# A new issue order, smaller first groups and a first chunk in two token halves, in a sketched attention with a rational activation

## The chip, the cores and the metric

The kernel runs on one core of a Trainium2 chip. The metric is the device time of one execution in microseconds, lower is better. Before the change it was 251.48 us, the median of three runs (251.42 to 254.35).

An execution profiled by the hardware gives the trace. Its span (248.8 us before) is a little shorter than the device time. The engines are called PE (matrix engine, TensorE), PEld (its weight loads), DVE (VectorE), ACT (ScalarE), POOL (GpSimd) and SP (the queue that issues most loads).

## The reference, cut to what matters

```python
def phi(x):                                   # attention with sketched features, r = 8
    a = np.einsum('rd,bhsd->bhsr', S1, x)
    b = np.einsum('rd,bhsd->bhsr', S2, x)
    return np.einsum('bhsi,bhsj->bhsij', a, b).reshape(*x.shape[:-1], r * r)
q_p, k_p = (phi(q), phi(k))                   # batch 4, heads 4, seq 1088, head_dim 32
kv  = np.einsum('bhsf,bhsd->bhfd', k_p, v)
num = np.einsum('bhsf,bhfd->bhsd', q_p, kv)
den = np.einsum('bhsf,bhf->bhs', q_p, np.sum(k_p, axis=2))[..., None] + 1e-06
x = num / den                                 # then 4352 tokens x 128
...
h = x @ w_in                                  # 128 -> 2048
P = a[0] + a[1] * h + a[2] * h2 + a[3] * h3
Q = 1.0 + np.abs(b[0]) * np.abs(h) + np.abs(b[1]) * h2
out = (P / (Q + 1e-06)) @ w_out               # 2048 -> 128
```

## The kernel before

The tokens are cut into nine chunks, eight of 512 tokens and a remainder of 256. For each chunk the queries' feature products, the division and a transpose give x; then 16 slices of 128 hidden columns are made. The slices are taken in groups, usually of eight, so that a group is 128 x 4096 elements in bfloat16. The rational function of a group is worked out in these steps:

```python
# PE:  h = w_in.T @ x, two slices (1024 columns) at a time;  ACT or DVE: hb <- h (cast, "e")
# DVE: u = |hb| (ab);  s = hb*hb (sq);           DMA or DVE: u += s             (us)
# DVE: t = a3*hb + a2 (hi);  t *= s (cu);  hb = a1*hb + a0 (lo);  DMA or DVE: t += hb   (ts)
# ACT: L = Ln(scale*u + 1);  u = Exp(-L)         (= 1/Q)
# DVE: t *= u (ov)                               (= P/Q)
# PE:  out += w_out.T @ t (pj)
```

A sum is either a DVE instruction or a DMA that accumulates, issued from GpSimd's queue. A table decides:

```python
def add(dst, src, name):
    d, s = T[dst, g][:, :gw], T[src, g][:, :gw]
    if ENGINE.get(name) == "DVE":
        nc.vector.tensor_add(out=d, in0=d, in1=s)
    else:
        nc.gpsimd.dma_start(out=d, in_=s, accum_op=AX.add, max_dma_last_dim=4096)
```

All work is a list of named steps. A fixed permutation, found by a search outside the kernel, says in which order the steps are issued; each engine then works through its own in that order:

```python
FIRST = [4, 4, 8]        # slices in the first chunk's groups;  LAST = [8, 4, 4] for the remainder
SKIP = ["f3"]
ORDER = [27, 4, 26, 30, 0, 36, ...]            # cut: 589 numbers
...
for i in order:
    s = self.steps[i]
    for key in s["take"]:
        self.slot[key] = free[key[0]].pop(0)   # a buffer of the pool
    s["fn"]()                                  # issues the instructions
```

Among the steps are dummy matmul pairs ("f0", "f1", ...), two products of 128 x 512 with zeros, 0.43 us a pair. They keep PE busy where it would stand still; a name in SKIP leaves one out.

## Time and profile before

| | before |
|---|---|
| device time, median of 3 | 251.48 us |
| span of the profiled run | 248.8 us |
| busy: PE, DVE, ACT | 222.5, 225.4, 213.7 us |
| first wide DVE operation / first logarithm | 24.68 / 32.59 us |
| last hidden matmul ends / last Exp ends | 217.3 / 243.1 us |

No engine is busy all the time and none is idle for long, so this table alone names no bound. The views have to be cut by time. The prediction shows the main cut. One more is needed, the stretches in which PE is full (start and end, length, busy time and count for PE, PEld, DVE, ACT, POOL, then granted clock, DMA share, GB/s):

```profile
50.00:110.00 60.00, 59.39 (x489) 33.49 (x490) 55.70 (x45) 54.26 (x40) 10.64 (x9) 1.00 0.99 192
110.00:200.00 90.00, 87.42 (x630) 46.22 (x629) 88.23 (x67) 86.68 (x59) 19.09 (x15) 1.00 0.97 178
```

PE has 0.6 us to spare from 50 to 110, while DVE and ACT have 4.3 and 5.7. From 110 to 200 the spare times are 2.6, 1.8 and 3.3. And at the end DVE waits for DMA sums (waits of DVE after 220 us: total us, times, longest):

```profile
DVE t L621 <- DMA t<-hb: 1.8, 4, 0.7
```

### The profile page before, as it was taken

The page shows a single profiled execution, that of the slowest core. Times are in us where ns is not written, and L with a number is a line of the kernel's source. Part 1 is how long each engine was busy: PE and PEld are TensorE (multiplying, and loading weights), DVE is VectorE, ACT ScalarE, POOL GpSimd, SP SyncE. Part 2 cuts the span into 40 slices and gives each one's busy share as a digit, 9 for nine tenths or more (in the row PEclk, how much of TensorE's full clock was granted, in tenths as well). Part 3 has the DMA queues.
Part 4 walks back from the last instruction along what each step waited for, and adds up shares of the span by engine and source line. Part 5 has one row for each costly group of instructions (what it writes and reads, how often), then busy time and mean ns, then how long its engine had stood idle before and what let it go on. Part 6 is the DMA issues. An engine that isn't in the chain of part 4 may idle for free.

```text
span 248.8 us, 4279 instructions
## 1 busy us (share of the span) xinstructions
PE 222.5 (89%) x1789; PEld 127.1 (51%) x1789; DVE 225.4 (91%) x205; ACT 213.7 (86%) x158; POOL 48.8 (20%) x61
## 2 busy tenths in 40 slices
PE   7999999999999999998999899999998969920763
PEld 2674455654636465553657354546453627720532
DVE  0785999998989989998999999999999999998993
ACT  3335589989989798989999999899999899899990
POOL 4000422132101212121111221122031312113210
PEclk9999999999999999999999999999999999995599
DMA  5994498999998899979999999999999999999982
GB/s 149 315 278 172 72 147 173 174 219 185 176 169 182 147 192 223 232 166 173 169 177 202 171 171 171 211 169 171 189 172 186 182 201 187 179 184 186 200 162 68
DMA packets 23427, 45.11 MB, mean 181 GB/s; under 512 B 5232, under 2 KB 13552, under 8 KB 23408
## 3 DMA queue, kind: packets, MB, share of 16 engines
q0 software_dynamic: 11232, 34.87, 79.7%
q1 hardware_dynamic: 11712, 9.90, 12.6%
q8 instruction: 14, 0.23, 0.4%
q10 hardware_dynamic: 464, 0.08, 0.2%
q14 instruction: 5, 0.04, 0.0%
HBM read 8.79 MB, written 2.23 MB: 44 GB/s over the span
## 4 chain that ended last, share of the span: by engine, by line
DVE 31%; PE 31%; DMA 20%; ACT 10%; issue 8%; SPq 0%; DVEq 0%; ACTq 0%; POOLq 0%
PE h_ps L572 15%; DMA u<-s 12%; DVE t L621 7%; DVE s L582 6%; DMA t<-hb 5%; DVE t L607 4%; DVE u L585 4%; PE h_ps L499 4%; ACT u L618 4%; DVE t L603 3%; PE out_ps L629 3%; ACT L L614 3%; DVE hb L610 2%; ACT hb L184 2%; DMA q<-in_q_dram 2%
## 5 line engine op out<-in xcount | busy, mean ns | idle before, releaser
L572 PE MATMUL h_ps<-xT,w_in_sb 128*128 128x512 f32 (+1 forms) x288 | 126.0, 577 | 4.2 <-ACT hb L184 2.7
L572 PEld LDWEIGHTS h_ps<-xT,w_in_sb 128*128 128x128 f32 x288 | 51.7, 190 | 56.5 <-issue 43.1
L184 ACT CAST hb<-h_ps 128x1024 bf16<-128x1024 f32 x66 | 64.8, 1020 | 8.2 <-PE h_ps L572 7.8
L614 ACT ACTIVATE L<-u,one_ap,lsc 128x4096 f32<-128x4096 bf16 (+2 forms) x20 | 65.9, 3295 | 6.4 <-DMA u<-s 6.3
L618 ACT ACTIVATE u<-L 128x4096 bf16<-128x4096 f32 (+2 forms) x20 | 62.3, 3116 | 0.2
L629 PE MATMUL out_ps<-w_out,t 128*128 128x128 bf16 x544 | 35.2, 225 | 15.8 <-DVE t L621 15.7
L594 POOL DMA_DIRECT2D u<-s x19 | 24.1, 1269 | 118.9 <-DVE u L585 54.5
L629 PEld LDWEIGHTS <-t 128*128 128x128 bf16 x544 | 32.5, 101 | 23.8 <-DVE t L621 20.6
L621 DVE TENSOR_TENSOR t<-t,u 128x4096 bf16<-128x4096 bf16 (+2 forms) x20 | 39.2, 1968 | 4.0 <-ACT u L618 2.2
L582 DVE TENSOR_TENSOR s<-hb 128x4096 bf16<-128x4096 bf16 (+2 forms) x20 | 39.2, 1963 | 1.5 <-ACT hb L184 1.5
L607 DVE TENSOR_TENSOR t<-t,s 128x4096 bf16<-128x4096 bf16 (+2 forms) x20 | 39.3, 1967 | 0.3
L594 POOL DMA_DIRECT2D t<-hb x18 | 21.6, 1200 | 72.2 <-issue 20.1
L610 DVE TENSOR_SCALAR hb<-hb,a_sb 128x4096 bf16<-128x4096 bf16 (+2 forms) x20 | 23.8, 1189 | 0.2
L603 DVE TENSOR_SCALAR t<-hb,a_sb 128x4096 bf16<-128x4096 bf16 (+2 forms) x20 | 23.6, 1183 | 0.0
L585 DVE TENSOR_SCALAR u<-hb 128x4096 int16<-128x4096 int16 (+2 forms) x20 | 22.3, 1115 | 0.1
L499 PE MATMUL h_ps<-qT,Srep 64*128 64x512 f32 (+1 forms) x72 | 19.5, 617 | 0.4 <-ACT hb L184 0.4
L506 DVE TENSOR_TENSOR q_pT<-A_sb,h_ps 128x1024 f32<-128x1024 f32 (+1 forms) x9 | 10.4, 1157 | 2.6 <-ACT A_sb L184 1.4
L519 PEld LDWEIGHTS h_ps<-kv,q_pT 128*64 128x64 f32 (+1 forms) x288 | 8.7, 134 | 5.1 <-issue 2.0
L519 PE MATMUL h_ps<-kv,q_pT 128*64 128x66 f32 (+1 forms) x288 | 10.1, 224 | 0.0
L184 ACT COPY A_sb<-h_ps 128x1024 f32<-128x1024 f32 (+1 forms) x9 | 8.7, 965 | 0.8 <-PE h_ps L499 0.8
L499 PEld LDWEIGHTS h_ps<-qT,Srep 64*128 64x128 f32 x72 | 5.4, 184 | 6.9 <-ACT hb L184 2.1
L184 ACT COPY kT<-h_ps 128x512 f32<-128x512 f32 x5 | 2.9, 585 | 5.3 <-PE h_ps L383 4.8
(89 smaller groups left out, 137.0 us busy)
## 6 DMA issues: line engine op xcount, KB each, us to landing
u<-s POOLq DMA_DIRECT2D x15, 1024.0 KB, 8.6
t<-hb POOLq DMA_DIRECT2D x15, 1024.0 KB, 9.5
k_sb<-in_k_dram SPq DMA_DIRECT2D x4, 512.0 KB, 4.3
q<-in_q_dram SPq DMA_DIRECT2D x8, 256.0 KB, 4.9
v<-in_v_dram SPq DMA_DIRECT2D x4, 512.0 KB, 8.2
out_dram<-oT SPq DMA_DIRECT2D x8, 256.0 KB, 7.0
w_in_sb<-in_moe_w_in_dram SPq DMA_DIRECT2D x2, 512.0 KB, 4.8
u<-s POOLq DMA_DIRECT2D x2, 512.0 KB, 7.7
```

Of the source, the lines that this page charges most:

```text
L184: nc.scalar.copy(out=out, in_=in_)
L499: nc.tensor.matmul(pair(i)[:, g, :W], lhsT=Srep[i][rows].rearrange("p g f -> p (g f)"), rhs=T["qT", n][rows, :W], start=True, stop=True)
L572: nc.tensor.matmul(p[:, i * W:(i + 1) * W], lhsT=w_in_sb[:, fi * 128:(fi + 1) * 128], rhs=T["xT", n][:, :W], start=True, stop=True)
L582: nc.vector.tensor_mul(out=new("s", g)[:, :gw], in0=h, in1=h)
L585: nc.vector.tensor_scalar(out=new("u", g)[:, :gw].bitcast(mybir.dt.int16), in0=T["hb", g][:, :gw].bitcast(mybir.dt.int16), scalar1=0x7FFF, ...
L594: nc.gpsimd.dma_start(out=d, in_=s, accum_op=AX.add, max_dma_last_dim=4096)
L603: nc.vector.tensor_scalar(out=new("t", g)[:, :gw], in0=T["hb", g][:, :gw], scalar1=a_sb[:, 3:4], scalar2=a_sb[:, 2:3], op0=AX.mult, op1=AX ...
L607: nc.vector.tensor_mul(out=T["t", g][:, :gw], in0=T["t", g][:, :gw], in1=T["s", g][:, :gw])
L614: nc.scalar.activation(out=new("L", g, l0)[:, :lw], in_=T["u", g][:, l0:l0 + lw], func=ACT.Ln, bias=one_ap, scale=lsc)
L618: nc.scalar.activation(out=T["u", g][:, l0:l0 + lw], in_=T["L", g, l0][:, :lw], func=ACT.Exp, scale=-1.0)
L621: nc.vector.tensor_mul(out=T["t", g][:, :gw], in0=T["t", g][:, :gw], in1=T["u", g][:, :gw])
L629: nc.tensor.matmul(T["out_ps", n][:, j * 128:(j + 1) * 128], lhsT=T["t", g][:, c:c + 128], rhs=W_out[:, fis[i], :], start=fis[i] == 0 and ...
```

## The change

The intent is to start the wide work earlier and to fit the steps together better. The first chunk is divided, transposed, evacuated and multiplied by its first two slices of w_in in two halves of 256 tokens; the first groups are 2, 2, 4 and 8 slices instead of 4, 4 and 8; a branch that no list used is removed; and the permutation, the table of engines and the buffers' homes are new. They come from a search outside the kernel.

```diff
-FIRST = [4, 4, 8]
+FIRST = [2, 2, 4, 8]
 ENGINE = {
...
-    "k31.ea": "DVE", "q7.ev": "DVE", "q8.xe": "DVE", "g1.ts": "DVE", "o0.eT": "DVE", "o1.eT": "DVE", "g7.e4": "DVE",
-    "o3.eT": "DVE", "o5.eT": "DVE", "g13.e4": "DVE", "g17.us": "DVE", "g18.ts": "DVE", "o8.eT": "DVE",
...
+    "k30.ea": "DVE", "k31.ev": "DVE", "q6.xe": "DVE", "q8.ev": "DVE", "q8.A": "DVE", "q8.xe": "DVE", "g1.us": "DVE",
+    "g1.ts": "DVE", "g6.e6": "DVE", "g17.us": "DVE", "o7.eT": "DVE", "g18.us": "DVE", "g20.us": "DVE",
+    "g20.ts": "DVE", "o8.eT": "DVE",
-FOUR = []
-SKIP = ["f3"]
+SPLIT = [0]
+SKIP = ["f2", "f10", "f8"]
 ORDER = [
-    27, 4, 26, 30, 0, 36, 1, 31, 6, 56, 20, ...      (cut: all 589 steps)
+    26, 30, 7, 1, 0, 27, 70, 71, 31, 32, 33, ...     (cut: all 604 steps)
...
+        if n in SPLIT:
+            out = []
+            for i in range(2):
+                s = plan.add(f"{nm}.dv{i}", "DVE", 830, lambda i=i: divide(i), ...)          (cut)
+                s = plan.add(f"{nm}.xt{i}", "PE", 250, lambda i=i: x_transposes(i), ...)     (cut)
+                out.append(add_copy(f"{nm}.xe{i}", lambda i=i: x_evac(i), W // 2, ...))      (cut)
+            return out
...
+            if n in SPLIT and fis[s] == 0:
+                hm = plan.add(f"{nm}.i{s}", "PE", 880, lambda s=s: h_mm(s, 0), ...)          (cut)
+                hm = plan.add(f"{nm}.h{s}", "PE", 880, lambda s=s: h_mm(s, 1), ...)          (cut)
```

Because the first chunk has one group more, a group g2 or later of the kernel before has a number one higher in the changed kernel. The last full group is g17 of the changed kernel and g16 of the one before.

## The prediction

> **What bounds the kernel now.** I read the page's busy table first, then busy time by stretch, then the chain of waits at the start, then the waits of each engine in the middle and at the end. The columns of the table are the busy time, its share of the span, and the number of instructions.
>
> ```profile
> PE 222.5 (89%) x1789; PEld 127.1 (51%) x1789; DVE 225.4 (91%) x205; ACT 213.7 (86%) x158; POOL 48.8 (20%) x61
> ```
>
> No single engine is the bound: three lie within 12 us of each other. Stretches separate them (start and end, length, busy time of each engine, granted clock, DMA share, GB/s):
>
> ```profile
> 0.00:24.68 24.68, 22.92 (x250) 13.62 (x251) 13.89 (x34) 9.69 (x15) 2.69 (x23) 1.00 0.75 230
> 24.68:50.00 25.32, 25.18 (x204) 13.96 (x204) 25.11 (x24) 20.95 (x22) 6.85 (x6) 1.00 0.87 142
> 50.00:220.00 170.00, 163.98 (x1232) 91.72 (x1232) 163.62 (x125) 160.23 (x109) 33.41 (x27) 1.00 0.98 184
> 220.00:243.10 23.10, 8.56 (x79) 6.30 (x80) 21.37 (x23) 22.86 (x13) 5.89 (x6) 0.70 0.99 185
> 243.10:248.80 5.70, 1.86 (x31) 1.52 (x28) 1.39 (x3) 0.00 (x0) 0.00 (x0) 1.00 0.16 46
> ```
>
> The cuts are chosen: 24.68 is where VectorE (DVE) begins its first wide operation, 243.10 is where ScalarE (ACT) finishes its last Exp. DVE is idle 24.68 - 13.89 = 10.8 us before the first wide operation, 0.2 in the second stretch, 6.4 in the third, 1.7 in the fourth, and 4.3 in the last. ACT is idle 15.0, 4.4, 9.8, 0.2 and 5.7. A narrower cut of the third stretch shows PE busy 59.4 of 60 us from 50 to 110 and DVE 107.9 of 110 from 110 to 220: the matrix engine sets the pace first, DVE afterwards, ACT in the last 23 us. The start is a chain, in order of time (start, length, what):
>
> ```profile
> 1.24 4.68 DMA q<-in_q_dram
> ...
> 11.16 2.48 PE h_ps L421 x80
> ...
> 15.10 1.09 PE h_ps L519 x32
> ...
> 17.70 0.59 PE h_ps L535 x4
> 18.29 1.06 PE h_ps L499 x4
> 19.35 0.62 PE w_ps L392 x16
> 19.97 7.08 PE h_ps L572 x16
> ```
>
> Two loads, then PE without a gap: the key sums (L421), the query sums (L519), the transposes of x (L535), and only after 1.7 us of the next chunk's work the first hidden matmuls (L572). In the middle ACT waits chiefly for one thing, the sum that a DMA makes before the logarithm; DVE waits for several small ones (total us, times, longest):
>
> ```profile
> ACT L L614 <- DMA u<-s: 5.7, 7, 1.2
> ACT hb L184 <- PE h_ps L572: 3.7, 6, 0.9
> ```
> ```profile
> DVE t L621 <- ACT u L618: 2.2, 4, 0.7
> DVE q_pT L506 <- PE h_ps L499: 1.2, 2, 0.7
> DVE den L526 <- PE h_ps L519: 1.1, 2, 0.7
> DVE a_t L186 <- PE w_ps L392: 1.0, 1, 1.0
> ```
>
> **What the Trainium skill says.** "Perfetto Trace Analysis", section "Optimization Strategy", says that the most-contended engine can change between regimes of a kernel, and that gaps should be looked for inside the regime concerned. The trace agrees: PE, then DVE, then ACT. "VectorE: DVE Perf Modes", section "The TRN2 errata", says that an instruction pays a fixed cost whatever its size, so cutting work smaller costs instructions. The trace agrees: the DVE product takes 2.285 us for 4096 columns, 1.215 for 2048 and 0.687 for 1024, a line with 0.16 us at zero. "DMA: Bandwidth & Descriptors", section "Issuing engines are not separate DMA queues", says that transfers of all issuers run on the same 16 engines and interleave. The trace agrees in that the DMA share is 0.98 in the middle while a 1 MB sum lands a median of 8.6 us (u) or 9.5 us (t) after issue; it rules nothing out.
>
> **The change part by part.** I read the built order of both programs.
>
> *Dead code.* The branch for FOUR is removed; its list was empty. Cost 0.
>
> *First chunk in halves, groups 2, 2, 4, 8.* One more group: three products at 0.16 us fixed, one absolute value at 0.15, two linear operations at 0.28 (0.807 us at 2048 columns against 0.543 at 1024), together +1.2 us on DVE; one more Ln and Exp, 0.38 + 0.20 = +0.6 on ACT. The divide in two adds one add, one reciprocal and one multiply of fixed cost, +0.5 on DVE; the second scaled evacuation +0.2 on ACT. Hidden matmuls in halves are neutral: 4 of 256 columns took 0.9 us against 1.72 for the whole pair.
>
> *Work moved between engines.* To DVE: three x evacuations (3 x 0.745), one cast (1.215), the remainder queries' two evacuations (0.43 + 0.68), one output (0.68), two small ones (0.98); and sums taken from DMA: one of 4096 columns (2.28), one of 2048 (1.22), four of 1024 (2.76). From DVE: one x (0.745), two casts (2.43), four outputs (2.73), two query copies (1.37), two small ones (0.71), sums of 2048, 2048 and 1024 (3.14). Net 12.5 - 11.1 = +1.4. With the parts above DVE gains 3.1 us of durations. Neighbours on DVE start about 0.07 us before the one ahead ends, and there are nine more instructions, so some +2.4 of time. ACT by the same count gets +1.4 + 0.8 = +2.2. DMA loses 5120 columns of sums, 1.3 MB of 34.9, nearly all in the last 40 us.
>
> *Start.* The loads begin with q1 (256 KB), then k0 (512), then q0 (256). From before: k0 landed near 4.9 and q0 near 5.9, so 256 KB take about 1 us; now k0 should land near 5.9 and q0 near 6.9. The keys' two transposes straddle q0's, w_in's second half and k1 go ahead of v0, and the key sums should start at 12.3 to 13.3 instead of 10.99. Then: key sums 2.7, an expansion 1.1 (which covers the two spread copies), first query sums to 16.6, x halves, g0's first half at 19.6, a transpose, q2 and q1's sums 1.9, g0's second half to 23.1, cast to 24.1. First wide DVE operation at about 24.4, against 24.68, with about the same DVE work behind it. So the halves give DVE almost nothing, because the loads take back what they save. ACT gains more: g1's sum is now on DVE, so its Ln can start after about 4.5 us of DVE work, near 29, against 32.59. That is some 2.5 us less idle ACT, about what its added work costs.
>
> *Middle.* Here the new order should pay. Between a group's last cast and its Ln, ACT has other work queued; I summed it from the order with the trace's durations (cast 1.02, Ln 3.81, Exp 3.63, copies 0.3 to 1.0). Over the ten full groups of chunks 3 to 7: mean 14.5 us before (13.1 to 17.6), 19.0 now (15.9 to 21.8). What must fit is DVE's absolute value and square (1.22 + 2.28) plus the landing (8.6, up to 12.4), 12 to 16 us: before falls short at times, as its seven waits show; now it rarely should. Most of the 5.7 us should go, and part of the 2.2 us behind it on DVE. From 24 to 110 us, where PE is full, five dummy matmul pairs (0.43 us each) stood in the order, now none: 2.2 us of PE, less about 1.3 lost at the start.
>
> *End.* DVE waited 1.8 us for the t sums; with 1.3 MB less to move I expect half. The 5.7 us from the last Exp to the end stay.
>
> *Sum.* ACT: +2.2 work, -2.5 start, -5 middle = -5. DVE: +2.4 work, 0 at the start, -3 of 6.4 in the middle, -1 at the end = -1.6. PE until 110: -0.9. The smallest gains decide, since each engine is the bound somewhere: about -1.9 us.
>
> **The rivals.** *A: added DVE work eats everything.* DVE is at 98% from 110 on, and takes a 2.28 us sum there. For: the stretch table. Against: 6 us of its idle time are still to be had. Result 251 to 253. *B: the ordering works throughout,* all ACT and most DVE waits vanish, and the start gains a microsecond because loads land sooner than I count. For: the 4.5 us of added distance. Against: DVE would need nearly no idle time outside start and end. Result 245 to 247. *C: the start gets worse,* v0 lands after 13.3 and all else shifts by 1 to 2 us. For: k1 and half of w_in before v0. Against: the share of DMA over the first 24.68 us was only 0.75. Result 251 to 252.5.
>
> **Range and chances.** 251.48 - 1.9 = 249.6. A and C bound it at 252.6, B at 246.3. Faster by over 2% (under 246.5) needs B nearly whole: 0.13. Slower by over 2% needs A and C together and more: 0.03. Within: 0.84.
>
> **What would show it.** First wide DVE operation at 24 to 25.5 us; first Ln at 28.5 to 30; key sums starting at 12 to 13.5; ACT's waits for u sums in the middle under 2 us; DVE busy 227.5 to 228.5, ACT near 216; DVE idle from 50 to 220 near 3.5. I am wrong if the waits for DMA stay (then slack was not their cause), if wide work starts before 23 us, or if DVE's time does not grow.

## The result and the profile after

| | before | after |
|---|---|---|
| median of the four runs each (range) | 251.45 (250.43 to 254.35) | 247.26 (246.79 to 248.07) |
| ratio of fast runs, 95% interval | | 0.985 (0.9807 to 0.9894) |
| span of the profiled run | 248.8 | 245.6 |

A ratio is the mean time of one kernel's fast runs over that of the other's of the same rounds, so it is not quite the ratio of the medians. Executions over 1.5% slower than the fastest of the same kernel are left out of the means. The gain is 1.5%: about 3.8 us by the ratio, 4.2 by the medians, 3.2 between the two spans. It counts as within 2%, and 247.26 lies inside the predicted range, below its middle.

The busy table and the stretches of the changed kernel follow. The cuts are at the same events as in the prediction's table (first wide DVE operation, 50, 220, last Exp's end):

```profile
PE 223.5 (91%) x1789; PEld 129.3 (53%) x1789; DVE 226.4 (92%) x215; ACT 215.5 (88%) x163; POOL 48.8 (20%) x60
```
```profile
0.00:25.07 25.07, 22.66 (x270) 14.75 (x271) 14.22 (x39) 9.48 (x15) 2.68 (x23) 1.00 0.75 228
25.07:50.00 24.93, 24.91 (x126) 12.19 (x124) 24.83 (x29) 21.66 (x22) 8.24 (x7) 1.00 0.88 146
50.00:220.00 170.00, 160.72 (x1258) 91.81 (x1253) 166.44 (x125) 164.35 (x117) 33.97 (x27) 0.99 0.98 184
220.00:240.16 20.16, 14.25 (x132) 10.01 (x133) 19.58 (x24) 19.96 (x11) 3.86 (x4) 0.77 0.76 148
240.16:245.60 5.44, 0.92 (x14) 0.57 (x11) 1.34 (x3) 0.00 (x0) 0.00 (x0) 0.76 0.10 24
```

Length less busy time is idle time, and the change of busy plus the changes of idle must come to the change of the span, for each engine. That is the whole account:

| us | DVE before | DVE after | ACT before | ACT after |
|---|---|---|---|---|
| busy | 225.4 | 226.4 | 213.7 | 215.5 |
| idle to the first wide DVE operation | 10.8 | 10.85 | 15.0 | 15.6 |
| idle from there to 50 | 0.2 | 0.1 | 4.4 | 3.3 |
| idle 50 to 220 | 6.4 | 3.6 | 9.8 | 5.65 |
| idle 220 to the last Exp | 1.7 | 0.6 | 0.2 | 0.2 |
| idle after it | 4.3 | 4.1 | 5.7 | 5.4 |
| span | 248.8 | 245.6 | 248.8 | 245.6 |

The start gave nothing to DVE and 0.5 us to ACT. The middle gave 2.8 us to DVE and 4.15 to ACT. The end gave DVE 1.3 us. The work itself grew by 1.0 and 1.7 us.

The start, first as the chain of waits (start, length, what), then as single instructions in order of time (start, length, engine, line, operation, tiles, and idle time before it with its releaser in brackets):

```profile
1.78 4.46 DMA q<-in_q_dram
12.07 2.69 PE h_ps L405 x80
22.92 6.21 PE h_ps L580 x16
```
```profile
25.07 0.43 DVE L593 TENSOR_SCALAR u<-hb 128x1024 int16<-128x1024 int16 x1
...
27.25 1.38 POOL L268 DMA_DIRECT2D w_out<-in_moe_w_out_dram  x1
...
27.65 1.23 DVE L611 TENSOR_SCALAR t<-hb,a_sb 128x1024 bf16<-128x1024 bf16 x1
...
30.58 1.24 ACT L622 ACTIVATE L<-u,one_ap,lsc 128x1024 f32<-128x1024 bf16 x1 [0.39 <-DVE u L600]
```

The key sums start at 12.07 in the chain (12.04 in the list of single instructions) instead of 10.99, one microsecond late as the loads' new order suggested. The first wide operation is 0.39 us later than before, not earlier. The first logarithm is at 30.58 instead of 32.59. It would have been sooner, but the linear operation at 27.65 took 1.23 us where the one at 26.01, of the same shape, took 0.54. At that time GpSimd was issuing the load of w_out. The kernel before shows the same thing in the same place: there an absolute value took 1.79 us instead of 0.69 beside the same issue (27.51 to 29.39).

The middle, as the waits of ACT from 50 to 220 us, then those of DVE (total us, times, longest):

```profile
ACT hb L187 <- PE h_ps L580: 3.0, 7, 1.0
ACT L L622 <- DMA u<-s: 1.7, 3, 0.9
```
```profile
DVE den L514 <- PE h_ps L503: 0.9, 3, 0.4
...
DVE q_pT L490 <- PE h_ps L483: 0.4, 1, 0.4
...
DVE t L629 <- ACT u L626: 0.2, 1, 0.2
```

ACT's waits for the sum ahead of the logarithm (L622, L614 before) fell from 5.7 to 1.7 us, and with them DVE's waits for the Exp (L629, L621 before) from 2.2 to 0.2. The time that a sum has did grow. Matched group by group in the two traces, the ten full groups of chunks 3 to 7 have 15.1 us from the last cast to the logarithm before (12.9 to 17.3) and 19.2 after (15.9 to 24.3). From the end of DVE's absolute value and square to the logarithm it is 9.2 and 12.3 us in the mean, while a u sum of 1 MB takes a median of 8.6 and 9.2 us to land. What ACT now waits for most is PE. The stretches in which PE was full:

```profile
50.00:110.00 60.00, 60.00 (x534) 34.41 (x529) 58.45 (x45) 58.10 (x47) 11.93 (x10) 1.00 1.01 192
110.00:200.00 90.00, 89.40 (x661) 49.90 (x660) 87.99 (x68) 86.28 (x61) 17.65 (x14) 1.00 0.96 178
```

PE is busy 149.4 of 150 us. It had been busy 146.8, and of that 2.2 us were the five dummy pairs that stood before 110 us and are gone (from 110 to 170 us three pairs stand now, and one stood before). The last hidden matmul ends at 212.1 instead of 217.3 us.

The end, as DVE's waits after 220 us. The wait for DMA sums, 1.8 us before, is not in it any more:

```profile
DVE oT L189 <- PE out_ps L637: 0.7, 1, 0.7
DVE t L629 <- ACT L L622: 0.6, 1, 0.6
```

### The profile page after: what moved, and what is told of

The parts are those of the page before. It is cut to its first block, busy times and chain, and to the rows that moved or that the text cites. A ratio compares the mean times of both kernels' runs of the same rounds, so it can differ in the third digit from the quotient of the medians.

```text
span 245.6 us, 4296 instructions
## 1 busy us (share of the span) xinstructions
PE 223.5 (91%) x1789; PEld 129.3 (53%) x1789; DVE 226.4 (92%) x215; ACT 215.5 (88%) x163; POOL 48.8 (20%) x60
## 4 chain that ended last, share of the span: by engine, by line
PE 56%; ACT 20%; DVE 9%; DMA 7%; issue 6%; SPq 0%; DVEq 0%; ACTq 0%
PE h_ps L580 33%; ACT u L626 9%; ACT L L622 8%; PE out_ps L637 6%; PE h_ps L483 5%; DMA u<-s 5%; PE h_ps L503 4%; ACT hb L187 3%; DVE t L629 2%; PE w_ps L405 2%; DVE s L590 2%; DMA q<-in_q_dram 2%; PE h_ps L405 1%; DVE t L611 1%; DVE u L593 1%
## 5 line engine op out<-in xcount | busy, mean ns | idle before, releaser
L580 PEld LDWEIGHTS h_ps<-xT,w_in_sb 128*128 128x128 f32 x292 | 52.5, 190 | 53.6 <-issue 45.4
L187 ACT CAST hb<-h_ps 128x1024 bf16<-128x1024 f32 x67 | 66.6, 1021 | 7.1 <-PE h_ps L580 6.6
L622 ACT ACTIVATE L<-u,one_ap,lsc 128x4096 f32<-128x4096 bf16 (+2 forms) x21 | 66.4, 3163 | 2.3 <-DMA u<-s 1.7
L637 PE MATMUL out_ps<-w_out,t 128*128 128x128 bf16 x544 | 36.1, 226 | 14.6 <-DVE t L629 14.6
L602 POOL DMA_DIRECT2D u<-s x17 | 22.0, 1296 | 95.8 <-DVE u L593 47.8
L602 POOL DMA_DIRECT2D t<-hb x19 | 23.3, 1242 | 87.9 <-ACT hb L187 33.3
L629 DVE TENSOR_TENSOR t<-t,u 128x4096 bf16<-128x4096 bf16 (+2 forms) x21 | 39.4, 1878 | 0.9 <-ACT L L622 0.6
L611 DVE TENSOR_SCALAR t<-hb,a_sb 128x4096 bf16<-128x4096 bf16 (+2 forms) x21 | 25.0, 1193 | 0.0
L593 DVE TENSOR_SCALAR u<-hb 128x4096 int16<-128x4096 int16 (+2 forms) x21 | 21.4, 1021 | 0.1
L483 PE MATMUL h_ps<-qT,Srep 64*128 64x512 f32 (+1 forms) x72 | 19.2, 614 | 0.0
L187 ACT COPY A_sb<-h_ps 128x1024 f32<-128x1024 f32 x8 | 8.1, 1014 | 0.9 <-PE h_ps L483 0.8
L517 DVE TENSOR_TENSOR x<-h_ps,den 128x512 f32<-128x512 f32 (+1 forms) x10 | 6.1, 611 | 0.3
```

The costliest lines, as they stand in the source:

```text
L187: nc.scalar.copy(out=out, in_=in_)
L483: nc.tensor.matmul(pair(i)[:, g, :W], lhsT=Srep[i][rows].rearrange("p g f -> p (g f)"), rhs=T["qT", n][rows, :W], start=True, stop=True)
L580: nc.tensor.matmul(p[:, i * W + c0:i * W + c1], lhsT=w_in_sb[:, fi * 128:(fi + 1) * 128], rhs=T["xT", n][:, c0:c1], start=True, stop=True)
L611: nc.vector.tensor_scalar(out=new("t", g)[:, :gw], in0=T["hb", g][:, :gw], scalar1=a_sb[:, 3:4], scalar2=a_sb[:, 2:3], op0=AX.mult, op1=AX ...
L622: nc.scalar.activation(out=new("L", g, l0)[:, :lw], in_=T["u", g][:, l0:l0 + lw], func=ACT.Ln, bias=one_ap, scale=lsc)
L629: nc.vector.tensor_mul(out=T["t", g][:, :gw], in0=T["t", g][:, :gw], in1=T["u", g][:, :gw])
```

## The experiments

The account says where idle time went, not which part of the change took it away. Four theories were to be told apart. The order: the new permutation leaves the sums more time. The dummies: five pairs off a full PE are worth their 2.2 us. The start: small first groups and token halves bring work forward. The end: sums taken from the DMA shorten the last stretch. All runs below were timed in five rounds against the kernel before; its medians in the three calls were 250.7, 250.42 and 250.33. All gave the right result. The changed kernel was not timed again in these calls, so a median set against its 247.26 us crosses calls; the ratios do not.

### Dummies out of the kernel before (b_nofill)

```diff
-SKIP = ["f3"]
+SKIP = ["f3", "f2", "f1", "f6", "f14", "f4"]
```

> The kernel before with the five dummy matmul pairs left out that stood before 110 us (f1, f2, f4, f6, f14); nothing else changed. Theory 'PE is the bound until 110 us, and the dummies are dead weight': up to 5 x 0.43 = 2.2 us of matrix work fall away, so 249.3 to 250.3 us against 251.45. Rival 'the gain is distance for the DMA sums and fewer stalls on ACT and DVE': 251.0 to 252.0, no change.

Measured: 252.99 us (251.83 to 256.21) with one slow run, 256.21, among the six; the five fast ones have a median of 252.32 (251.83 to 254.08). Ratio 1.0067 (1.0016 to 1.0119). Taking out 2.2 us of useless work made it slower. A line of PE's waits from 50 to 110 us shows one reason:

```profile
PE h_ps L487 <- DMA q<-in_q_dram: 2.5, 1, 2.5
```

PE came to a chunk's queries before they had landed, and it had not waited there before. The load had left at 88.33 us, 0.9 us sooner than before, but its last pieces landed near 105.3 us instead of 100.7. The granted clock from 50 to 110 us was 0.97 instead of 1.00. The waits for u sums stayed (4.0 us from 110 to 220, 4.6 with the dummies). So leaving the dummies out did not help by itself. But the run does not show that PE had room to spare: until 100 us PE was busy 97.6 us, against 97.5 with four dummy pairs (1.7 us) among them. It was ahead by the length of the dummies, and lost that again in the one wait at 105 us. What their room would be worth in the old order without this wait is not shown.

### Dummies into the changed kernel (a_fill)

```diff
-FILLS = 16
+FILLS = 18
-SKIP = ["f2", "f10", "f8"]
+SKIP = []
 ORDER = [   (cut: five dummy pairs placed between 50 and 110 us)
```

> The changed kernel with five dummy matmul pairs put back at about the places where the kernel before had them. Theory 'dead weight on a bound PE': 248.5 to 249.5 us against 247.3. Rival 'PE has room, the gain is elsewhere': 247.0 to 247.8.

Measured: 249.80 us (249.69 to 250.26), ratio 0.9954 (0.9914 to 0.9993), span 248.0. The five pairs last 2.15 us; the span grew by 2.4.

```profile
50.00:110.00 60.00, 59.88 (x512) 33.43 (x508) 56.24 (x44) 55.61 (x44) 11.23 (x10) 1.00 0.99 188
110.00:200.00 90.00, 89.59 (x685) 49.98 (x683) 87.90 (x69) 86.39 (x62) 17.65 (x14) 1.00 0.94 176
```

PE is as full as without them, and DVE and ACT do 2.2 and 2.5 us less work from 50 to 110. In the changed kernel PE sets the pace from 50 to 110 us and pays for every extra matmul there. For the kernel before, b_nofill leaves it open whether the same holds. That the new order leaves these five pairs out is therefore worth some 2 us within it, but not shown to be worth as much in the old one.

### The old start before the new rest, and the reverse (old_head, new_head)

The edit of old_head takes groups, engines and order of the kernel before up to the first hidden matmul of chunk 1, near 38 us, and those of the changed kernel from there; new_head does the reverse at the same place.

```diff
 # old_head, against the changed kernel
-FIRST = [2, 2, 4, 8]
+FIRST = [4, 4, 8]
-SPLIT = [0]
+SPLIT = []
 ORDER, ENGINE, HOME   (cut: old until 38 us, new afterwards)
```

> The order, groups, engines and loads of the kernel before up to the first hidden matmul of chunk 1 (some 38 us), without token halves; from there the new order and engines. Theory 'the order of the rest pays': 246.8 to 248.5 us, that is all or most of the gain stays. Rival 'the halves and the small first groups pay': 250.5 to 252.

> The mirror of the last run: token halves, groups of 2, 2, 4, 8 and the new order up to the same point, then the order and engines of the kernel before. Theory 'the order of the rest pays': 250.5 to 252.5 us. Rival 'the halves and the small first groups pay': 247.3 to 248.5. If the parts add, this gain and that of the run with the old head make up 4.2 us.

Measured: old_head 249.3 us (248.56 to 250.21), ratio 0.9933 (0.9891 to 0.9975); new_head 254.71 us (253.44 to 255.7), ratio 1.0135 (1.0085 to 1.0185). If the parts were independent the two gains would multiply to the whole one; instead 0.9933 x 1.0135 is 1.0067, not 0.985. The reason is at the seams: two halves of two searches do not leave the engines at the same place. One line each of the waits behind the seam, old_head from 50 to 80 us and new_head from 36 to 75:

```profile
ACT hb L184 <- PE h_ps L577: 3.0, 1, 3.0
```
```profile
ACT kv L450 <- PE w_ps L403: 3.9, 1, 3.9
```

These stalls are in neither kernel. Past its seam old_head runs like the changed kernel (last hidden matmul at 213.3 us), and new_head has 4.5 us of ACT's waits for u sums from 110 to 220 again. That fits the theory of the order, and so do the other runs: from 110 to 220 us these waits are 4.6, 4.0 and 4.5 us with the old order (the kernel before, b_nofill, new_head), and at most 1.1 us in each of the nine kernels that keep the new order there (the changed one, a_fill, old_head, a_nofill, a_nosplit, a_both, a_448, a_448b, a_sumdma_b). But neither ratio can be read as the worth of a part.

### Three dummy pairs fewer in the changed kernel, and no token halves (a_nofill, a_nosplit, a_both)

```diff
 # a_nofill
-SKIP = ["f2", "f10", "f8"]
+SKIP = ["f2", "f10", "f8", "f6", "f5", "f1"]
 # a_nosplit; a_both has both edits
-SPLIT = [0]
+SPLIT = []
-    "q0.xT.1": "h_ps",
+    "q0.xT": "h_ps",
 ORDER   (cut: the halves' steps merged, the rest as it was)
```

> The changed kernel without the three dummy matmul pairs that stand between 110 and 170 us (f6, f5, f1). If the matrix engine is the bound there, as the five pairs added in an earlier run suggest (2.2 us of dummies cost 2.5), up to 3 x 0.43 = 1.3 us go: 246.0 to 247.0 against 247.3, and it would beat both kernels. Rival, from the run without dummies in the kernel before (0.7% slower, a stall on a query load): 247.3 to 248.5.

> The changed kernel with the first chunk's x in one piece again: one divide, one set of transposes, one scaled evacuation, one first pair of hidden matmuls, each at the place of the second half in the order. My theory, that the halves give nothing because PE has no gap there: within 0.5 us of the changed kernel, 246.8 to 247.8. Rival, the halves bring the first wide operation forward: 248 to 249.5.

> The changed kernel without token halves and without the three dummy pairs of the middle: both runs alone were level with it or 0.3 us faster. If the two small gains add: 246.0 to 246.8, ratio about 0.982 of the kernel before. If both were noise: 246.8 to 247.4.

Measured: a_nofill 246.93 us (246.29 to 247.2), ratio 0.9836 (0.9792 to 0.988); a_nosplit 247.07 (246.76 to 247.79), 0.9849 (0.98 to 0.9898); a_both 247.28 (246.61 to 247.56), 0.9849 (0.9804 to 0.9894). The first two had medians 0.2 to 0.3 us below that of the changed kernel, and so were tried together; together they gave nothing. The differences are not told apart from noise, and no version was found that clearly beats the changed kernel. So of the 1.3 us that the three pairs between 110 and 170 us take on PE, no more than 0.3 shows in the medians: the full price that a_fill found from 50 to 110 us is not seen in that stretch, though the intervals are too wide to rule it out.

The halves are therefore worth nothing that could be seen. The trace of a_nosplit shows why: the first hidden matmuls begin at 21.92 us instead of 20.15, but in one piece, and the wide work starts when it did with the halves, at 24.98 instead of 25.07:

```profile
24.98 0.43 DVE L592 TENSOR_SCALAR u<-hb 128x1024 int16<-128x1024 int16 x1 [0.85 <-ACT hb L186]
```

### First groups of 4, 4, 8 in the changed kernel (a_448, a_448b)

```diff
-FIRST = [2, 2, 4, 8]
+FIRST = [4, 4, 8]
 ENGINE   (a_448: + "g0.us": "DVE";  a_448b: + "g0.ts": "DVE", sum u of g0 by DMA, ahead of w_out)
 ORDER    (cut: the steps of g0 and g1 merged, the rest as it was)
```

> The changed kernel with its first two groups of 2 slices made one group of 4 (4, 4, 8 as before), its parts at the places of the second group, with one sum on DVE and one by DMA as those two had between them. Theory 'small first groups are worth little': 246.8 to 248.0. Rival 'the early start of ACT (first Ln at 30.6 us against 32.6) is what was gained': 248.5 to 250.

Measured: 250.76 us (250.25 to 251.72), ratio 0.9998 (0.9952 to 1.0043). This run does not test what it should. With no sum ahead of it in GpSimd's queue, the load of w_out left at the start:

```profile
3.41 1.32 POOL L265 DMA_DIRECT2D w_out<-in_moe_w_out_dram  x1
...
15.47 2.08 PE L402 MATMUL h_ps<-v,k_p 128*64 128x64 f32 x64 [0.37 <-DVE a_t L186]
```

It took transfer time from keys and queries. The DMA share of the first 25 us was 0.93 instead of 0.75, and the key sums began at 15.47 instead of 12.04. So 3.4 us of the 3.5 lost can be the load's. A second try kept a sum ahead of the load:

> The first groups 4, 4, 8 again, without the flaw of the earlier run: there the load of w_out came first in GpSimd's queue and ran against the first loads, and everything started 3.4 us late. Now the first group's u sum is a DMA ahead of w_out, and its Ln stands where the later of the two small groups had it; the t sum is on DVE. Theory 'small first groups are worth little, because PE sets the pace until 200 us': 247.0 to 248.3. Rival 'ACT's early start is what was gained': 248.8 to 250.5.

Measured: 248.33 us (248.08 to 250.27), ratio 0.9908 (0.9854 to 0.9961), span 247.2, 1.6 above the changed kernel's. From 20 to 55 us two waits stand in it, one for DVE and one for ACT:

```profile
ACT L L619 <- DMA u<-s: 3.2, 2, 1.6
...
DVE u L590 <- ACT hb L184: 1.7, 1, 1.7
```

In the changed kernel ACT waited 0.7 us for such sums in that stretch. The small first groups are worth about a microsecond: 1.1 by the medians, 1.6 by the spans, 1.4 by the ratios; the intervals of the two ratios overlap. The spans say too much: in this profile q0 landed at 7.14 us instead of 6.24 and the key sums began at 12.80 instead of 12.04, and nothing in the edit comes ahead of that.

### The last full group's u sum back to the DMA (a_sumdma, a_sumdma_b)

```diff
 ENGINE = {
...
-    "g17.us": "DVE",
 ORDER   (a_sumdma: right behind its square;  a_sumdma_b: later, behind g16.us and g15.ts)
```

> The changed kernel with the last full group's sum (u<-s, 4096 columns) made by a DMA again, as in the kernel before, issued right behind the square. Theory 'moving sums off the DMA was not what paid': DVE busy 2.2 us less, time 246.5 to 248.0. Rival 'the DMA queue at the end was the bound, relief of 1 MB paid': 249 to 251.

Measured: 259.18 us (259.03 to 260.15), ratio 1.0335 (1.0288 to 1.0381). The waits from 205 us on:

```profile
POOL u L600 <- ACT L L620: 16.4, 1, 16.4
DVE t L627 <- DMA t<-hb: 13.9, 1, 13.9
ACT L L620 <- DMA u<-s: 10.2, 1, 10.2
```

GpSimd's queue is worked in order. The sum placed at its head could not be issued until a logarithm had ended; GpSimd issued nothing for 16.4 us, and the sum of the group before stood behind it. In the changed kernel that sum left at 201.19 us; here both left together at 210.51. ACT waited 10.2 us for it. So this run measures a place in a queue, not the worth of a DMA sum. The second try puts the sum behind the older ones:

> The last full group's u sum by DMA again, now issued behind the u sum of the group before it and the t sum, so that it cannot block them (in the earlier run it stood ahead and ACT waited 10 us). Theory 'the sum taken from the DMA was not what paid': 246.5 to 248.0. Rival 'at the end the DMA queue is the bound, and 1 MB less of it paid': 249 to 251.

Measured: 249.61 us (248.89 to 250.37), ratio 0.9947 (0.9901 to 0.9992), span 247.8, 2.2 above the changed kernel's. The last hidden matmul ends at the same time (212.2 us, against 212.1). The loss is all behind it, in DVE's waits from 205 us on:

```profile
DVE t L627 <- DMA t<-hb: 4.6, 4, 3.0
```

The changed kernel has no such wait there. So moving one 4096-column sum to DVE was worth some 2.3 us (2.35 by the medians, 2.2 by the spans), although DVE is then busy 2.0 us more (226.4 against 224.4).

### The old end behind the new rest (old_tail)

The edit is the order and the engines of the changed kernel until the division of chunk 6, near 160 us, and those of the kernel before, with its dummies, from there.

```diff
-SKIP = ["f2", "f10", "f8"]
+SKIP = ["f3"]
 ORDER, ENGINE, HOME   (cut: new until 160 us, old afterwards)
```

> The changed kernel up to the divide of chunk 6 (some 160 us), from there the order and engines of the kernel before, its DMA sums at the end included. Theory 'the order of the first 160 us pays, since PE is full there': 247.5 to 249.0, the seam costing up to a microsecond. Rival 'the end pays': 249.8 to 251.5.

Measured: 251.89 us (251.23 to 254.53), ratio 1.005 (0.9989 to 1.011). Until 160 us it is the same as the changed kernel, but for small differences (PE is busy 157.1 us, against 157.5). The last hidden matmul ends at 217.9 instead of 212.1 us; a line of PE's waits from 160 to 220 us shows most of that, and below it the same line of the kernel before:

```profile
PE h_ps L578 <- ACT hb L185: 4.6, 3, 2.3
```
```profile
PE h_ps L572 <- ACT hb L184: 2.3, 1, 2.3
```

By its time this run says that all of the gain is in the end. Of the 4.6 us, one wait of 2.3 (at 204.05 us) is the old end's own: the kernel before has it at 203.42 us, and in the changed kernel these waits come to 1.1. The other 2.2 us, 1.75 of them at 166.57 us, stand in neither kernel, so they are the cost of the splice, and the run cannot be read as the worth of the end. The kernel before was not ahead at 160 us either: PE's useful work until then (busy time less dummies at 0.43 us a pair, 155.62 - 2.15 before and 157.46 - 1.29 after) is 2.7 us further in the changed kernel.

### How the runs compare with what was expected

Of the twelve runs, a_nofill, a_nosplit, a_both and a_sumdma_b fell into one of the ranges set down for them. old_head (249.3) and a_448b (248.33) fell between the two. b_nofill, new_head, a_448, a_sumdma, old_tail and, by 0.3 us, a_fill came out slower than both. a_448 and a_sumdma measured something else than was meant. In b_nofill and new_head, and in part in old_tail, the trace shows a wait that the edit itself brought.

## Why the prediction was right, and where its steps were not

**Total.** Predicted 249.6 us with 246.3 to 252.6 as the range and 84% for a change within 2%; it was 247.26, and within 2%. The direction was right, and so was the place where most idle time went, the middle. The size was taken too small: -1.9 us was predicted, and -3.2 came in span, -3.8 by the ratio.

**How the sum was formed.** The three sums, -5 for ACT, -1.6 for DVE and -0.9 for PE until 110 us, could not all hold: the account table shows that each engine's busy and idle changes come to the same span. Leaning to the smaller ones was the right instinct, but the -1.9 is none of the three, and its working does not say how it came from them. PE's was the furthest off. Until 110 us PE's useful work came out 2.2 us further, not 0.9 (107.49 - 2.15 before, 107.58 after): the start lost 0.5 us instead of 1.3, and 0.6 us of idle time from 50 to 110 went too. By 160 us it was 2.7 us. PE's waits from 50 to 160 us, 2.3 before, are all gone, which the prediction had not counted.

**DVE's work, the mis-sized term.** The durations grew by 3.1 us in the prediction and by 2.8 in the trace (236.0 to 238.8, overlaps counted twice). The failed step is the next one, "Neighbours on DVE start about 0.07 us before the one ahead ends, and there are nine more instructions, so some +2.4 of time". That counted an overlap for the new instructions only (there are ten, not nine), and left the old neighbours as they were. Measured, 128 of 204 pairs of neighbours overlapped before by 10.6 us in all, and 152 of 214 now by 12.4. A neighbour that needs the result of the one ahead starts about 0.03 us after its end, an independent one mostly 0.08 us before it. The new order has more pairs of the second kind. So busy time grew by 1.0 us, not 2.4, and DVE was busy 226.4 us, below the 227.5 to 228.5 that was to show. This one term is 1.4 us off (0.3 in the durations, 1.1 in the overlap), and the whole sum missed the span by 1.3.

**The start.** The key sums (12 to 13.5 predicted, 12.04 measured) and the first wide operation (24 to 25.5, measured 25.07) came as worked out, and DVE gained nothing. k0 and q0 landed at 5.4 and 6.2 us, sooner than the 5.9 and 6.9 of the prediction. But "the halves give DVE almost nothing, because the loads take back what they save" has a wrong reason in it: a_nosplit shows that with the same loads the halves save nothing. ACT's start is a second mis-sized term. The first logarithm was put at 28.5 to 30 us and came at 30.58. 0.7 us of this is the linear operation that took 1.23 us beside the issue of w_out, a collision that the trace of before had shown in the same place and that I had not looked for. ACT's idle time to 50 us fell by 0.5 us, not 2.5. That did no harm, since DVE's account had nothing from it. The small groups are worth about one microsecond in the run that merged them again; the prediction gave them no net gain.

**The middle.** Right in mechanism and nearly in size. ACT's waits for u sums were to fall under 2 us and fell to 1.7; DVE's idle time was to be near 3.5 and was 3.6; ACT's fell by 4.15, where 5 was taken. The distance from a group's last cast to its logarithm, 14.5 and 19.0 us by the count from the order, is 15.1 and 19.2 in the traces. That this distance is the cause is supported by the waits going with the order in every run, as said above; no run changed the distance alone.

**The end.** DVE's waits for t sums were to halve from 1.8 us; none is left after 220 us. DVE's idle time there fell by 1.3 us where 1 was predicted. What the prediction did not see is that this depends on the sum that was moved: with it back on the DMA, 2.2 us of span return. Rival A, that the added DVE work eats the gain, is refuted for that sum by a_sumdma_b.

**The rivals.** A (251 to 253) did not come. C (251 to 252.5) did not come either, as v's sums started before 13.3. B (245 to 247) was nearer than the central estimate, but only in part for its reasons: most waits for sums went, but the start gained DVE nothing, and DVE kept 3.6 us of idle time in the middle.

**What stays open.** Single undoings gave about 1.2 us for the small groups, 2.3 for the last sum, 0 for the halves and nothing clear for the dummies that are left. The five dummy pairs gone before 110 us, the other moved sums and copies, and the buffers' new homes have no clean run of their own. They need not add up: they come to 3.5 of the 3.8 us, while the account puts most of the idle time saved into the middle. A saving there reaches the end only if nothing is lost behind it, as a_sumdma_b loses 2.2 us. How the gain divides between the middle and the end can't be settled by splices of these two orders, since each of the three made a stall of its own at the seam.

## What to carry to other kernels

Where three engines are nearly full, make the account of busy and idle time for each engine and stretch; the sums must agree, and a term that only one engine gains is not yet a gain in time. Whether filler work on a full engine is free depends on the rest of the order, so test it in both directions, as b_nofill and a_fill do, and look in the trace whether the edit brought a new wait, which spoilt b_nofill. In a kernel with a fixed issue order, an edit also moves its neighbours in a queue that works in order; check what now stands at the queue's head (here a load that left too early cost 3.4 us, and a sum that could not leave cost 10.2) before reading the run as a test of the edit.

## What the Trainium skill lacked or had wrong

- "VectorE: DVE Perf Modes", section "The DRAIN you can't avoid", says that the next operation does not start until the pipe empties, and then that one which is not held starts earlier. That section gives no size for it. Here 152 of 214 pairs of neighbours on DVE overlapped, by 0.08 us in the mean and 12.4 us in all, while dependent ones started about 0.03 us after the end of the one ahead. The prediction knew a size (0.07 us) but took it for the added instructions only, some 0.7 us; the overlap grew by 1.8.
- "Perfetto Trace Analysis", section "Identifying the Most-Contended Engine", would judge the matrix engine's headroom by its weight loads' busy share and its FLOPs rather than by matmul busy time. Here weight loads were busy 96.5 of 175 us from 25 to 200 us (55%), which looks like room, and matmuls 174.4; and 2.15 us of dummies added from 60 to 104 us cost 2.4 us. There matmul busy time was the better sign; the share by FLOPs was not worked out. But taking 1.3 us of dummies out between 110 and 170 us gained 0.3 by the medians, within noise, so that neither sign decides without a run.
- "SBUF — State Buffer", section "SBUF: two separate sides", describes the port pair that DVE and GpSimd share as a lock by which whichever starts first blocks the other, but for a DMA that GpSimd issues it warns of one direction only, DVE holding up the issue. The traces show the other: a DVE operation took 1.23 us instead of 0.54 (1.79 instead of 0.69 in the kernel before) while GpSimd issued the load of w_out. In each of the 13 kernels that issue this load beside DVE work, one DVE operation begun during the issue took 0.35 to 1.1 us longer than its like, and no other in the trace did; in a_448, where the load left at 3.41 us, none did. The sums that GpSimd issued did not do it: from 26.41 to 27.41 us it issued one, and DVE's operation took 0.55. That the lock is the cause was not tested.
